# Loads over all 128 partitions: x, the rearranged Wo and the turned rows of a fused attention and gated-MLP kernel

## The chip, the cores and the metric

The kernel runs on one core of one Trainium2 chip. The metric is the device time of one execution in microseconds (us); the median over several runs counts. A core has five engines that run side by side: TensorE (PE, matrix multiplications; its weight loads are listed as PEld), VectorE (DVE), ScalarE (ACT), GpSimd (POOL) and SyncE (SP, which here only issues DMAs). Sixteen DMA engines move data between DRAM and on-chip memory (SBUF, 128 partitions). A DMA is issued by SP, ACT or POOL into that issuer's queue.

## The reference

Inputs are x (1 x 2048 x 640), wqkv (640 x 1920), wo (640 x 640), w_gate and w_up (640 x 1536) and w_down (1536 x 640), all bf16. The second x of the signature is not used.

```
xn = layernorm(x)
q, k, v = split(xn @ wqkv)                # 32 heads of 20
scores = q @ k^T * 20**-0.5               # causal, window of 256
a = (softmax(scores) @ v) @ wo
m = (sigmoid(xn @ w_gate) * (xn @ w_up)) @ w_down
out = x + a + m
```

## The kernel before

The 2048 rows are worked on in four chunks of 512 (`NCH`, `CW`); a chunk has four blocks of 128 rows (`SBC`). For a chunk the kernel needs the normalized rows with the model dimension on the partitions, `xnT[c]` (128 partitions x 4 blocks x 5 slices x 128 rows). The projections (`proj_block` for q and k, `both_v` and `project_v` for v) and the gate and up products (`g_gu`) all multiply with it.

Chunk 0 comes by four loads ahead of everything (`load_rows`) and is turned by TensorE. Chunks 1 to 3 go another way. `load_x(c)` loads the raw rows into a tile `xc` by four DMAs, DVE takes the statistics of each block (`ln_block`), POOL makes the reciprocal deviations (`rstds`), DVE normalizes in place and transposes squares of 32 x 32 (`turn_block`) into a tile `turn`. `turn_rows(c)` then finishes the turn through DRAM: it stores `turn` to a DRAM tile and loads `xnT[c]` from it, five DMAs on SP's queue. So that the 32 x 32 squares come out in the right place, `load_x` puts 32 consecutive rows of each block of 128 on each quarter of the partitions.

The output weights Wo are needed in an order of heads that differs from the input's. `turn_wo(r, side)` copies them piece by piece from DRAM to a DRAM tile `wo_i` by DMAs on POOL's queue (eight pieces of 80 rows), and `load_wo` loads the result into `wo`.

The heads' rows of q and k pass through DRAM as well: each projected block is copied from PSUM to a tile `st` (six buffers; DVE copies q, ACT copies k), stored to `scratch` (names sq and sk in the profile) and loaded in another layout (`spread`, tiles qT and kT). `clear` zeroes the padding rows of the scratch on POOL's queue; a small POOL copy, `landed`, reads the first loaded chunk 1 tile, so that the two clears are issued after that load.

TensorE's order is static. An outer loop walks the attention steps (scores of a step, L500; exponential on ACT, L506; masks on POOL and DVE; weighted values, L533, two steps later). Between them a planner (`Fill`) pulls other work from a list of labelled parts with their costs: gate and up products, projections of the next chunk, down projection and output (`g_out`: `down`, `add_wo`, `add_x`). DVE's share of the next chunk's normalization (`g_norms`) is mixed into these parts; `turn_rows(2)` and `load_x(3)` are reached while chunk 0's output is made. PSUM tiles of all these products rotate through four banks (`ps_d`). `new_rows` loads the rows of x that `add_x` adds (tile `rows`, three buffers).

SP works through its DMA issues in program order and waits at each for what that DMA needs. `load_x(1)` is issued ahead of chunk 0's q and k stores, `load_x(2)` among chunk 1's k stores, `turn_rows(2)` and `load_x(3)` ahead of two output stores and the rows of the third block.

Of the kernel before, what the change touches and what calls it, by code (L numbers as in the profile page):

```python
# [9 lines left out]
P = 128  # L10
S = 2048
D = 640
H = 32
DH = 20
F = 1536
DC = D // P
FC = F // P
CW = 512
NCH = S // CW
SBC = CW // P  # L20
HG = 4
NG = H // HG
# [13 lines left out]
BF16 = mybir.dt.bfloat16  # L36
# [33 lines left out]
def kernel(  # L70
# [11 lines left out]
    nc = tc.nc  # L82
    x2 = A_x.flatten_outer_dims()
# [27 lines left out]
    xc = {}  # L111

    def load_x(c):
        t = xp.tile([P, SBC, D], BF16, name="xc")
        xc[c] = t
        rows = x2[c * CW:(c + 1) * CW, :].rearrange("(a n t) d -> a t n d", a=SBC, n=SBC)
        for a in range(SBC):
            nc.sync.dma_start(out=t[32 * a:32 * a + 32], in_=rows[a])

    wqkv = const.tile([P, DC, 3 * D], BF16, name="wqkv")  # L120
    wqkv_r = A_wqkv.rearrange("(c p) n -> p c n", p=P)
# [3 lines left out]
    wo = const.tile([P, DC, D], BF16, name="wo")  # L125
# [28 lines left out]
    def clear(w):  # L154
        rows = scratch[w].rearrange("(h j) s -> h (j s)", j=32)[:, DH * CW:]
        nc.gpsimd.dma_start(out=rows.rearrange("h (a e) -> h a e", a=4), in_=zero[:, 0:3, :])
# [14 lines left out]
        for lo, hi in ((0, 3), (3, 6), (6, 8), (8, 10), (10, FC)):  # L171
            nc.sync.dma_start(out=wd[:, lo:hi, :], in_=wd_r[:, lo:hi, :])

    wo_i = tc.dram_tile([HG, NG * DH, D], BF16, name="wo_i")

    def turn_wo(r, side):
        to = wo_i.rearrange("i (r a d) n -> r a i (d n)", a=2, d=DH)
        rows = A_wo.rearrange("(a r i d) n -> r a i (d n)", a=2, i=HG, d=DH)
        nc.gpsimd.dma_start(out=to[r, side].rearrange("i (e w) -> e i w", e=16),
                            in_=rows[r, side].rearrange("i (e w) -> e i w", e=16))  # L180

    def load_wo():
        for i in range(HG):
            nc.sync.dma_start(out=wo[32 * i:32 * i + 32, :, :],
                              in_=wo_i[i].rearrange("(m j) n -> j m n", j=32))


    ident = const.tile([P, P], BF16, name="ident")
# [13 lines left out]
    xnT = {}  # L202
# [33 lines left out]
    turns = {}  # L236
# [8 lines left out]

    def turn_rows(c):
        xnT[c] = xtp.tile([P, SBC, DC, P], BF16, name="xnT")
        rows = tc.dram_tile([HG, P, D], BF16, name=f"turn{c}")
        nc.sync.dma_start(out=rows.rearrange("g p e -> p g e"), in_=turns[c].rearrange("p (g e) -> p g e", g=HG))
        for g in range(HG):  # L250
            nc.sync.dma_start(out=xnT[c][32 * g:32 * g + 32].rearrange("p a m t -> p a (m t)"),
                              in_=rows[g].rearrange("(a j) e -> j a e", j=32))

# [91 lines left out]
    def g_norms(c, turn):  # L347
        got = []
        yield from g_stats(c, got)
        yield 0  # L350
        for s in range(SBC):
            norm_rows(c, s, *got)
            yield 0
            turn_block(c, s)
            if turn and s == SBC - 1:
                turn_rows(c)
            yield 0
# [3 lines left out]
    def g_first(rstds):  # L361
        for s in range(0, SBC, 2):
            norm_rows(1, s, mvs1, rstds)
            norm_rows(1, s + 1, mvs1, rstds)
            yield 0
        for s in range(SBC):
            turn_block(1, s)
            if s == SBC - 1:
                turn_rows(1)
            yield 0  # L370
# [81 lines left out]
    def new_rows(c, s, name="rows", bufs=3, queue=nc.sync):  # L452
        rows = lnp.tile([P, D], BF16, name=name, bufs=bufs)
        queue.dma_start(out=rows, in_=xr[:, c * SBC + s, :])
        return rows
# [242 lines left out]
    banks.close()  # L698
    ps_s = banks.enter_context(tc.tile_pool(name="ps_s", bufs=1, space=bass.MemoryType.PSUM))
    load_x(1)  # L700
    load_gu(wg, B_w_gate, 0, FS // 2)
    landed = const.tile([P, 2], BF16, name="landed")
    nc.gpsimd.tensor_copy(out=landed, in_=xc[1][:, 0, 0:2])
    clear("q")
    clear("k")
    for k, _ in enumerate(g_qk(0)):
# [11 lines left out]
    def later(load, *args):  # L718
        load(*args)
        yield 0  # L720

    behind1 = {("qk"[n // 4], 1 + n % 4): (lambda n=n: turn_wo(n // 2, n % 2)) for n in range(2 * NP)}
    behind1["k", 0] = lambda: load_x(2)
    norms2 = itertools.chain(g_norms(2, True), later(load_x, 3))
    norms3 = g_norms(3, False)
    fill.add("gu0a", mix(g_gu(0, 0, 6), g_first(rstds1), 0), 6 * GU)
# [3 lines left out]
    fill.add("v1", mix(g_v(1), norms2, 2, 1, False), 40 * 136)  # L730
    fill.add("rest1", later(spread_rest, 1), 0)
    fill.add("wo", later(load_wo), 0)
    fill.add("gu0c", mix(g_gu(0, 9, 12), norms2, 0, 1, False), 3 * GU)
    fill.add("gu1a", mix(g_gu(1, 0, 2), norms2, 0, 1, False), 2 * GU)
    fill.add("out0", mix(g_out(0, g_gu(1, 2, 3)), norms2, 1, 1), OUT + GU)
    fill.add("qk2", mix(g_qk(2), norms3, 2, 1, False), 50 * MM)
    fill.add("v2", g_v(2), 40 * 136)
    fill.add("gu1b", mix(g_gu(1, 3, 12), norms3, 0, 2), 9 * GU)
    fill.add("turn3", later(turn_rows, 3), 0)
    fill.add("out1", g_out(1, g_gu(2, 0, 1)), OUT + GU)  # L740
    fill.add("qk3", g_qk(3), 50 * MM)
# [39 lines left out]
    c = NCH - 1  # L781
# [5 lines left out]
    rows = [new_rows(c, s, queue=nc.scalar) for s in range(SBC - 1)]  # L787
# [58 lines left out]
```

## Time and profile before

| what | value |
|---|---|
| median of 3 runs | 308.87 us (308.83 to 309.37) |
| the profiled execution | 309.65 us, of it span 308.0 us |
| TensorE clock granted | 1.00 |
| PE busy | 302.9 us, 98% of the span |
| DVE, ACT, POOL busy | 184.4, 193.2, 83.8 us |
| DMA | 36.86 MB, 120 GB/s over the span |
| xc loads, xnT loads, wo loads: median time from issue to landing | 4.0, 3.4, 9.1 us |

The span is the time from the first to the last instruction in the profile; the execution's own time lies 1.65 us above it. Times of single instructions are microseconds from the span's start. In a timeline a line reads: start, duration of the merged stretch, engine, line of the kernel, operation, what is written and read, how many, and in brackets the idle time ahead with what ended it. In a list of waits it reads: who waited, for whom, then the total in us, how many times, and the longest. In the DMA lines a queue has packets, megabytes, and the time that its packets took as a share of sixteen engines in the stretch asked for. The row of DMA digits gives the busy share of the DMA engines in 40 equal slices, in tenths.

### The profile page before, as it was taken

Reading aid. Unit: us, or ns where it says so; the run is one execution under the profiler, and the core shown is the slowest. Engines: PE = TensorE matmul, PEld = TensorE weight load, DVE = VectorE, ACT = ScalarE, POOL = GpSimd, SP = SyncE. Lnnn points to the kernel's source line nnn. Section 1 sums busy time; section 2 is a strip of 40 time slices with the busy share of each in tenths; the row PEclk is TensorE's granted clock in tenths of the full one; section 3 lists DMA queues with packets and bytes.
Section 4 is the critical chain, followed back from the end, with each engine's and each line's share of the span. In section 5 each row is a group of like instructions: output and inputs, shape, how many; then the busy total and the mean of one; then the engine's idle time right before and its main releaser. Section 6 shows DMA issues by size and latency. Waiting matters only on the chain.

```text
span 308.0 us, 10147 instructions
## 1 busy us (share of the span) xinstructions
PE 302.9 (98%) x4431; PEld 168.2 (55%) x4431; DVE 184.4 (60%) x378; ACT 193.2 (63%) x183; POOL 83.8 (27%) x189
## 2 busy tenths in 40 slices
PE   7999999999999999999999999999999999999996
PEld 3654445564456655654456655644546765444774
DVE  5787449298984579577642666454383627465523
ACT  6923785977766458867655557777766466778000
POOL 5011234635314133422213122241314132221100
PEclk9999999999999999999999999999999999999999
DMA  7997739889927222721152113550000210000301
GB/s 213 347 306 238 266 102 309 220 248 320 198 94 199 85 72 93 228 80 47 43 128 72 39 65 99 163 192 2 3 2 2 70 41 23 2 2 2 88 21 64
DMA packets 35756, 36.86 MB, mean 120 GB/s; under 512 B 2944, under 2 KB 35456, under 8 KB 35712
## 3 DMA queue, kind: packets, MB, share of 16 engines
q1 hardware_dynamic: 34304, 33.84, 36.6%
q0 software_dynamic: 544, 1.61, 1.7%
q10 hardware_dynamic: 864, 0.77, 0.9%
q8 instruction: 34, 0.56, 0.8%
q14 instruction: 10, 0.08, 0.1%
HBM read 25.59 MB, written 11.44 MB: 120 GB/s over the span
## 4 chain that ended last, share of the span: by engine, by line
PE 97%; DMA 1%; ACT 1%; DVE 0%; issue 0%; SPq 0%
PE pg L414 18%; PE y L437 18%; PE pu L423 17%; PE pqk L266 15%; PE ps L500 9%; PE y L444 7%; PE acc L533 6%; PE pv L324 6%; PE pv L304 1%; DMA xc<-in_A_x_dram 1%; PE pvh L304 0%; PE pt L233 0%; ACT turn L640 0%; ACT turn L645 0%; DVE turn L651 0%
## 5 line engine op out<-in xcount | busy, mean ns | idle before, releaser
L506 ACT ACTIVATE pT<-ps 128x2048 bf16<-128x2048 f32 x75 | 140.8, 1877 | 56.0 <-PE ps L500 33.4
L489 POOL TENSOR_SCALAR_AFFINE_SELECT pT<-pT 64x256 bf16<-64x256 bf16 (+1 forms) x126 | 67.5, 536 | 181.0 <-ACT pT L506 122.9
L414 PE MATMUL pg<-xnT,wg 128*128 128x512 bf16 x240 | 59.9, 380 | 0.0
L423 PE MATMUL pu<-xnT,wu 128*128 128x512 bf16 x240 | 59.8, 380 | 0.0
L427 DVE SCALAR_TENSOR_TENSOR h<-th,pu 128x512 bf16<-128x512 f32 x48 | 32.9, 685 | 42.8 <-ACT th L417 25.7
L437 PE MATMUL y<-wd,h 128*128 128x320 bf16 (+2 forms) x396 | 56.8, 295 | 0.0
L266 PE MATMUL pqk<-xnT,wqkv 128*128 128x512 bf16 x200 | 45.8, 381 | 0.0
L437 PEld LDWEIGHTS <-h 128*128 128x128 bf16 x396 | 36.8, 98 | 15.9 <-issue 2.3
L517 DVE TENSOR_TENSOR pT<-pT,keep 128x512 bf16<-128x512 bf16 (+2 forms) x81 | 35.4, 444 | 15.6 <-ACT pT L506 14.7
L417 ACT ACTIVATE th<-pg 128x512 f32<-128x512 f32 x48 | 28.6, 595 | 20.2 <-PE pg L414 19.9
L423 PEld LDWEIGHTS <-wu 128*128 128x128 bf16 x240 | 22.3, 98 | 27.3 <-issue 2.2
L414 PEld LDWEIGHTS <-wg 128*128 128x128 bf16 x240 | 21.7, 98 | 26.4 <-issue 2.9
L266 PEld LDWEIGHTS <-wqkv 128*128 128x128 bf16 x200 | 22.6, 119 | 19.0 <-issue 1.5
L500 PE MATMUL ps<-qT,kT 20*64 20x320 bf16 (+4 forms) x1440 | 32.0, 260 | 0.0
L544 DVE STREAM_TRANSPOSE t<-acc 128x512 f32<-128x512 f32 x32 | 21.0, 694 | 17.9 <-PE acc L533 17.9
L448 DVE SCALAR_TENSOR_TENSOR rows<-y,rows 128x320 bf16<-128x320 f32 x30 | 14.4, 489 | 24.2 <-PE y L444 24.2
L500 PEld LDWEIGHTS <-kT 20*64 20x64 bf16 x1440 | 13.5, 103 | 27.2 <-issue 26.7
L444 PE MATMUL y<-wo,oc 128*128 128x320 bf16 (+2 forms) x165 | 24.2, 295 | 0.0
L533 PE MATMUL acc<-pT,v 64*32 64x320 bf16 (+4 forms) x1440 | 20.3, 253 | 0.5 <-issue 0.5
L533 PEld LDWEIGHTS <-v 64*32 64x32 bf16 x1440 | 17.0, 92 | 4.2 <-issue 1.6
L444 PEld LDWEIGHTS <-oc 128*128 128x128 bf16 x165 | 15.5, 98 | 6.7 <-issue 1.0
L324 PE MATMUL pv<-wqkv,xnT 128*64 128x320 bf16 x240 | 17.4, 300 | 0.0
(61 smaller groups left out, 173.3 us busy)
## 6 DMA issues: line engine op xcount, KB each, us to landing
qT<-sq SPq DMA_DIRECT2D x16, 256.0 KB, 4.2
kT<-sk SPq DMA_DIRECT2D x16, 256.0 KB, 4.3
xc<-in_A_x_dram SPq DMA_DIRECT2D x16, 160.0 KB, 4.0
sq<-st SPq DMA_DIRECT2D x20, 128.0 KB, 3.6
sk<-st SPq DMA_DIRECT2D x20, 128.0 KB, 2.9
out_dram<-rows SPq DMA_DIRECT2D x15, 160.0 KB, 1.8
wg<-in_B_w_gate_dram SPq DMA_DIRECT2D x4, 480.0 KB, 7.2
wu<-in_B_w_up_dram SPq DMA_DIRECT2D x4, 480.0 KB, 7.4
```

Source lines behind the costliest of these rows:

```text
L266: nc.tensor.matmul(ps, lhsT=wt[:, m, :], rhs=xnT[c][:, :, d, :], start=(d == 0), stop=(d == DC - 1))
L324: nc.tensor.matmul(ps[hf * U:(hf + 1) * U, 0:HALF], lhsT=xnT[c][:, s, d, rows], rhs=wqkv[:, d, 2 * D + hf * HALF:2 * D + (hf + 1) * HALF], ...
L414: nc.tensor.matmul(pg, lhsT=part(wg, d, f), rhs=xnT[c][:, :, d, :], start=(d == 0), stop=(d == DC - 1))
L423: nc.tensor.matmul(pu, lhsT=part(wu, d, f), rhs=xnT[c][:, :, d, :], start=(d == 0), stop=(d == DC - 1))
L427: nc.vector.scalar_tensor_tensor(out=h, in0=th, scalar=1.0, in1=pu, op0=ADD, op1=MULT)
L437: nc.tensor.matmul(y[:, 0:cut[1] - cut[0]], lhsT=ht[c, f][:, s * P:(s + 1) * P], rhs=wd[:, f, cut[0]:cut[1]], start=(f == 0), stop=False)
L444: nc.tensor.matmul(y[:, 0:cut[1] - cut[0]], lhsT=oc[c, m][:, s * P:(s + 1) * P], rhs=wo[:, m, cut[0]:cut[1]], start=False, stop=(m == DC - 1))
L489: nc.gpsimd.affine_select(out=part, in_=part, pattern=pattern, compare_op=GE, fill=0.0, base=-1 if sign > 0 else 0, channel_multiplier=sign)
L500: nc.tensor.matmul(ps[side * U:(side + 1) * U, i, col * U:(col + n) * U], lhsT=qk["k", kc, half][32 * i:32 * i + DH, 2 * r + side, kb * U: ...
L506: nc.scalar.activation(out=pt[:, :, 0:used, :], in_=ps[:, :, 0:used * U], func=EXP, scale=SCALE)
L517: nc.vector.tensor_tensor(out=part, in0=part, in1=limit.to_broadcast([P, HG, n * U]), op=MIN)
L533: nc.tensor.matmul(accs[side][32 * i:32 * i + 32, q * U:(q + n) * U], lhsT=vt[sb][rows, b, at:at + 32], rhs=pt[rows, i, col:col + n, :], s ...
```

## The change

Four functions are edited and one line that reads a loaded tile.

- `load_x`: the four DMAs each filled 32 partitions with four stretches of 32 rows; now each fills one of the four column blocks on all 128 partitions.
- `turn_rows`: one store of `turn` over 128 partitions and four loads of 32 partitions; now four stores, one for each column group, and one load over 128 partitions.
- `turn_wo` and `load_wo`: `wo_i` now has the rows in the order in which `wo` wants them, so that `wo` is loaded by two DMAs over 128 partitions and not by four over 32. A piece of 20 rows that crosses a border of 32 is split, which makes 12 DMAs of the 8.
- `landed` reads the last column block of the tile, and so waits for the fourth DMA.

```diff
     def load_x(c):
         t = xp.tile([P, SBC, D], BF16, name="xc")
         xc[c] = t
-        rows = x2[c * CW:(c + 1) * CW, :].rearrange("(a n t) d -> a t n d", a=SBC, n=SBC)
-        for a in range(SBC):
-            nc.sync.dma_start(out=t[32 * a:32 * a + 32], in_=rows[a])
+        rows = x2[c * CW:(c + 1) * CW, :].rearrange("(a n t) d -> n a t d", a=SBC, n=SBC)
+        for n in range(SBC):
+            nc.sync.dma_start(out=t[:, n, :], in_=rows[n])
...
-    wo_i = tc.dram_tile([HG, NG * DH, D], BF16, name="wo_i")
+    wo_i = tc.dram_tile([D, D], BF16, name="wo_i")
 
     def turn_wo(r, side):
-        to = wo_i.rearrange("i (r a d) n -> r a i (d n)", a=2, d=DH)
-        rows = A_wo.rearrange("(a r i d) n -> r a i (d n)", a=2, i=HG, d=DH)
-        nc.gpsimd.dma_start(out=to[r, side].rearrange("i (e w) -> e i w", e=16),
-                            in_=rows[r, side].rearrange("i (e w) -> e i w", e=16))
+        to = wo_i.rearrange("(m i j) n -> m i (j n)", i=HG, j=32)
+        rows = A_wo.rearrange("(a r i d) n -> r a i (d n)", a=2, i=HG, d=DH)[r, side]
+        at, end = (2 * r + side) * DH, (2 * r + side + 1) * DH
+        first = at
+        while at < end:
+            m, j = divmod(at, 32)
+            n = min(end - at, 32 - j)
+            e = 16 if n == DH else n
+            nc.gpsimd.dma_start(
+                out=to[m][:, j * D:(j + n) * D].rearrange("i (e w) -> e i w", e=e),
+                in_=rows[:, (at - first) * D:(at - first + n) * D].rearrange("i (e w) -> e i w", e=e))
+            at += n
 
     def load_wo():
-        for i in range(HG):
-            nc.sync.dma_start(out=wo[32 * i:32 * i + 32, :, :],
-                              in_=wo_i[i].rearrange("(m j) n -> j m n", j=32))
+        rows = wo_i.rearrange("(m p) n -> p m n", p=P)
+        for lo, hi in ((0, 3), (3, DC)):
+            nc.sync.dma_start(out=wo[:, lo:hi, :], in_=rows[:, lo:hi, :])
...
     def turn_rows(c):
         xnT[c] = xtp.tile([P, SBC, DC, P], BF16, name="xnT")
-        rows = tc.dram_tile([HG, P, D], BF16, name=f"turn{c}")
-        nc.sync.dma_start(out=rows.rearrange("g p e -> p g e"), in_=turns[c].rearrange("p (g e) -> p g e", g=HG))
+        rows = tc.dram_tile([SBC * P, D], BF16, name=f"turn{c}")
+        to = rows.rearrange("(a g j) e -> g a j e", a=SBC, g=HG)
         for g in range(HG):
-            nc.sync.dma_start(out=xnT[c][32 * g:32 * g + 32].rearrange("p a m t -> p a (m t)"),
-                              in_=rows[g].rearrange("(a j) e -> j a e", j=32))
+            nc.sync.dma_start(out=to[g], in_=turns[c][:, g * D:(g + 1) * D])
+        nc.sync.dma_start(out=xnT[c].rearrange("p a m t -> p a (m t)"), in_=rows.rearrange("(a p) e -> p a e", p=P))
...
-    nc.gpsimd.tensor_copy(out=landed, in_=xc[1][:, 0, 0:2])
+    nc.gpsimd.tensor_copy(out=landed, in_=xc[1][:, SBC - 1, 0:2])
```

## The prediction

> **What bounds the kernel now.** I read the page first (busy time, the chain that ended last, the DMA lines), then TensorE's waits, then the DMA issues in time order, then the instructions that wait for them.
>
> From the page: busy time, the chain, the packets.
>
> ```profile
> PE 302.9 (98%) x4431; PEld 168.2 (55%) x4431; DVE 184.4 (60%) x378; ACT 193.2 (63%) x183; POOL 83.8 (27%) x189
> DMA  7997739889927222721152113550000210000301
> DMA packets 35756, 36.86 MB, mean 120 GB/s; under 512 B 2944, under 2 KB 35456, under 8 KB 35712
> PE 97%; DMA 1%; ACT 1%; DVE 0%; issue 0%; SPq 0%
> ```
>
> TensorE's own waits, in full:
>
> ```profile
> PE pwarm L199 <- PEq L830: 0.8, 1, 0.8
> PE pt L233 <- DVE turn L651: 0.7, 1, 0.7
> PE acc L533 <- issue: 0.5, 1, 0.5
> ```
>
> The end is set by TensorE at 97%, and after the start it waits for no DMA at all. So no faster load can shorten the run: its gain is capped near 0, while a transfer that grows past its slack costs its full excess. The DMA digits show little slack in the first 31 us and from 46 to 85 us (8 and 9 tenths).
>
> The edited transfers on SP's queue (start, time, what), and the packets' share of 16 engines in two stretches: the turn store alone (89 to 93 us), then four xnT loads with two rows loads (153 to 160):
>
> ```profile
> 10.28 1.76 SPq L118 DMA_DIRECT2D xc<-in_A_x_dram  x4
> 31.96 0.37 SPq L249 DMA_DIRECT2D turn<-turn  x1
> 37.70 2.99 SPq L251 DMA_DIRECT2D xnT<-turn  x4
> 97.34 0.43 SPq L454 DMA_DIRECT2D rows<-in_A_x_dram  x1
> q1 hardware_dynamic: 528, 0.66, 45.7%
> q1 hardware_dynamic: 864, 0.98, 58.7%
> ```
>
> The store over 128 partitions: 0.457 x 16 x 4 us = 29.2 us for 512 packets of 1280 B (16 more are end marks), 57 ns each. The second: 65.7 us, less 256 rows packets at 57 ns and 96 marks at about 10 ns, leaves 50 us for 512 packets into 32 partitions, 98 ns each. That is what the change can gain: 41 ns a packet, if sixteen engines still share it.
>
> **What the change does to each transfer.** Page: 2944 packets under 512 B. The issue list has 168 transfers; 168 x 16 = 2688, and the two smallest last stores (48 and 32 KB) add 128 + 128 short rows: 2944. So every transfer of before ended with a small mark from each of 16 engines. All had 16, 32 or 128 as outermost count on both sides. The wo_i stores, outermost count exactly 16, appear in the packet records as 1600 and 4800 B, together one index of that count per engine. The new x loads and turn stores count a = 4 outermost in DRAM (a, then 32 rows). No row shows such a count. Bounds: still 16 engines, or one share per index, 4 engines. I take 4, because the nearest row, wo_i, was handed out by whole indices and 4 leaves four.
>
> [...]
>
> With 4 engines, a group of four 160 KB transfers is 512 / 4 = 128 packets on each of the same four, and everything behind it in those queues waits. I take 60 ns a packet, just above 57 since neighbours are loaded: 7.7 us a group; bounds 55 and 98 ns, 7.0 and 12.5 us.
>
> **Place 1, load_x(1).** Who waits:
>
> ```profile
> POOL landed L703 <- DMA xc<-in_A_x_dram: 14.5, 1, 14.5
> ACT st L272 <- DMA sq<-st: 1.5, 1, 1.5
> 21.69 1.76 ACT L272 CAST st<-pqk 128x512 bf16<-128x512 f32 x3 [1.48 <-DMA sq<-st]
> 23.75 1.24 PE L414 MATMUL pg<-xnT,wg 128*128 128x512 bf16 x5
> ```
>
> Before, wu (issued at 6.5, 9.8 to landing) was in at 16.3 and the last x load at 19.1, just ahead of POOL's copy at 19.2: 2.8 us. Now 7.7, so what follows is 4.9 us late. The sq stores queue behind; ACT's copy of the second k block waits for the first sq store because st has six buffers, and its PSUM bank is the one that pg at 23.75 takes. That copy ends at about 22.3, a slack of 1.45. Stall: 4.9 - 1.45 = 3.4 us. With the clears' packets (2 us), now beside the sq stores, up to 5.4; at 55 ns with engines that are free earlier, 1.4.
>
> **Place 2, turn_rows(1).** The first user of the turned rows:
>
> ```profile
> 45.48 1.24 PE L266 MATMUL pqk<-xnT,wqkv 128*128 128x512 bf16 x5
> ```
>
> DVE follows TensorE, so the stores issue near 35.4. Ahead of them in the queues stand six qT/kT/wu/wg loads, before drained at 36.1; they move by about the 4.5 us of the late k stores, to 40.6. Four stores take 7.7 where one took 1.6: 48.3. The single load then costs what the lone 640 KB turn store did, 3.2 us from issue (four xnT loads: 5.4): 51.7 with the issue. Against 45.48 TensorE is then 6.2 us late in all, place 1 included.
>
> **Place 3, turn_rows(2) and load_x(3).**
>
> ```profile
> 102.69 0.88 DVE L448 SCALAR_TENSOR_TENSOR rows<-y,rows 128x320 bf16<-128x320 f32 x2
> 108.38 2.35 PE L266 MATMUL pqk<-xnT,wqkv 128*128 128x512 bf16 x10
> ```
>
> In times of before: stores from 89.9 end at 97.6 (92.2), the load at 101.0 (98.4), the x group at 108.7 (100.6), and the out store and rows load behind it (8 packets an engine each) at 109.6 (101.4). DVE wants those rows at 102.69: 6.9 late. Its first result, 0.49 later, frees the bank that pqk takes at 108.38, a slack of 5.2: 1.7 us more. DVE's masks stand behind that wait, but pv needs them only at 114.7.
>
> **What costs nothing.** load_x(2) at 56.5 ends 4 to 5 us later, near 67; its statistics run on DVE from 65.5 to 71.4, one block per load, and chunk 1's first scores at 78.0 have 6 us left. The SP queue behind, wd included, moves about 3 us; wd landed at 74.5 to 77.2 and is first used at 82.8, so at 7 us of delay this cover is gone and each further us costs one. wo is 640 packets over 128 partitions, 40 per engine: 40 x 41 ns = 1.6 us earlier and two issues fewer, against the 3 us; it landed at 86.1 and is used at 89.1, so 0 to 1 us. Turning Wo takes 12 POOL issues for 8: 4 x 0.53 = 2.1 us of POOL between 50 and 61 us, ahead of selects whose pv is two steps away; POOL is 27% busy. turn_rows(3) stores at 144.4 and its load waited until 153.7 anyway: covered up to 9 us. SP's issue count in turn_rows stays five. `landed` now waits for the fourth load alone, which is the last.
>
> **The sum.** 6.2 + 1.7 = 7.9 us. The profiled execution took 309.65 (span 308.0), so 317.55 for it; the median of the three runs is 0.78 below it: 308.87 + 7.9 = 316.8.
>
> **Rivals.** *Sixteen engines all the same* (not slower). The x group takes 32 x 57 ns = 1.8 us for 2.8, xnT and wo land earlier, and TensorE, which waits for none of it, does not notice: 308.9. For it: all 168 transfers used 16. Against: none had an outermost count of 4. It decides wherever a group stays under 2.8 + 1.45 = 4.3 us, 33 ns a packet on four engines, which no 1280 B row reaches.
>
> *The four engines get in each other's way.* Each then owns a block of 32 partitions, and 32 partitions is where the 98 ns rows come from. At 12.5 us a group: place 1 costs 9.7 - 1.45 = 8.3; place 2: queues drain 9.7 later than 36.1, stores to 58.3, load 61.5, 16.0 late in all; place 3 is 16.5 - 5.2 = 11.3: +27.3, 336. Against it: those rows had 16 engines on one block, not one. [...]
>
> *Slack swallows most*: four engines at 55 ns, no clears in the way. Place 1 1.4; place 2 drains 2.5 later (38.6), stores to 45.6, load 49.3, 3.8 late in all; place 3 nothing: 312.7. For it: many of these queues idle in between. Against: the 9s of the first 31 us.
>
> **How the numbers follow.** Chances: forecast 0.52; sixteen engines 0.12 (0.02 of it faster, since 0.5 us of issue idle could go; 0.09 the same, 0.01 slower); collision 0.18, spread over 320 to 336; slack 0.18, 0.02 of it the same. The forecast weighs most because whole indices are what the nearest row shows and 60 ns lies by the 57 of a transfer over all partitions. The range leaves out the sixteen engines, the last 0.02 and the collision's upper third, some 0.2: 311 to 331. Faster 0.02, same 0.11, slower 0.87; the bound is 0.2%, 0.6 us, about what a measurement of this kernel can tell from no change.
>
> **What would show it.** Small packets: the new kernel has 170 transfers, 2720 marks and 256 short rows on sixteen engines, 2976; on four, the 12 x loads and 12 turn stores lose 12 marks each: 2688. TensorE's waits should list pg or pqk with microseconds, xc landings of 9 us and more at 10.3, turn stores of 8 to 10 us, and DVE's rows waiting near 103. If the small packets count 2976 and xnT lands sooner, the four-engine step is wrong and with it the sign; if the marks are fewer and TensorE still waits for nothing, the slacks are.

## The result, and the profile after

The changed kernel takes 320.69 us (median of 6 runs, 317.97 to 321.7); the kernel before, run beside it, 308.94 (6 runs, 308.82 to 309.37). The ratio is 1.037, 95% interval 1.0327 to 1.0413: slower by 11.75 us. The profiled execution of the changed kernel took 317.97 (span 315.9), 8.3 above the profiled one of before. Of the six runs this is the only one with a granted clock of 1.000; the others have 0.984 to 0.995.

From the page of the changed kernel: busy time, the packets, and the chain that ended last.

```profile
PE 303.1 (96%) x4431; PEld 168.1 (53%) x4431; DVE 183.9 (58%) x378; ACT 192.8 (61%) x183; POOL 86.3 (27%) x193
DMA packets 35500, 36.86 MB, mean 117 GB/s; under 512 B 2736, under 2 KB 35184, under 8 KB 35456
PE 83%; DMA 10%; DVE 4%; SPq 2%; ACT 1%; issue 0%; DVEq 0%; ACTq 0%
```

TensorE does the same work (303.1 us busy, 302.9 before), but 10% of the chain is now DMAs. The packets under 512 B fell from 2944 to 2736, although there are two more transfers (170 for 168). All of TensorE's waits that are new, from its list of waits:

```profile
PE pqk L274 <- DVE rows L456: 3.3, 1, 3.3
PE pqk L274 <- DMA xnT<-turn: 2.7, 1, 2.7
PE pg L422 <- ACT st L280: 1.4, 1, 1.4
PE pu L431 <- DMA wu<-in_B_w_up_dram: 0.6, 1, 0.6
```

Together 8.1 us. With the 0.5 us of issue idle gone and 0.2 us more busy time that is 7.8 of the 7.9 us by which the span grew. They stand at the three places of the prediction. The SP queue there (start, time, what), and who waited, from the timelines:

```profile
10.31 4.36 SPq L118 DMA_DIRECT2D xc<-in_A_x_dram  x4
33.59 4.58 SPq L259 DMA_DIRECT2D turn<-turn  x4
45.77 0.37 SPq L260 DMA_DIRECT2D xnT<-turn  x1
108.38 0.43 SPq L462 DMA_DIRECT2D rows<-in_A_x_dram  x1
```

```profile
23.14 0.18 POOL L711 COPY landed<-xc 128x2 bf16<-128x2 bf16 x1 [18.43 <-DMA xc<-in_A_x_dram]
24.75 2.05 ACT L280 CAST st<-pqk 128x512 bf16<-128x512 f32 x4 [4.49 <-DMA sq<-st]
115.67 0.89 DVE L456 SCALAR_TENSOR_TENSOR rows<-y,rows 128x320 bf16<-128x320 f32 x2 [8.46 <-DMA rows<-in_A_x_dram]
116.22 2.32 PE L274 MATMUL pqk<-xnT,wqkv 128*128 128x512 bf16 x10 [3.33 <-DVE rows L456]
```

Place 1: the x group lands at 23.1 (19.2 before), ACT's copy waits for the sq store until 24.75 (21.69). Place 2: from the first turn store to the load behind the four, 33.6 to 45.8. Place 3: DVE waits 8.5 us for rows and passes 3.3 on to TensorE.

How many engines worked can be read directly. Chunk 2's four stores are alone on SP's queue from 95.5 to 103.8 us, and the packets' share of sixteen engines there is

```profile
q1 hardware_dynamic: 527, 0.65, 23.9%
```

0.239 x 16 = 3.8 engines. All four transfers had been issued by 97.0, and still no more than four engines were at work, so the four share the same ones.

### The profile page after: what moved, and what is told of

Read it like the earlier page. It is cut to its first block, busy times and chain, and to the rows that moved or that the text cites. A ratio compares the mean times of both kernels' runs of the same rounds, so it can differ in the third digit from the quotient of the medians.

```text
span 315.9 us, 10142 instructions
## 1 busy us (share of the span) xinstructions
PE 303.1 (96%) x4431; PEld 168.1 (53%) x4431; DVE 183.9 (58%) x378; ACT 192.8 (61%) x183; POOL 86.3 (27%) x193
## 2 busy tenths in 40 slices
DMA packets 35500, 36.86 MB, mean 117 GB/s; under 512 B 2736, under 2 KB 35184, under 8 KB 35456
## 4 chain that ended last, share of the span: by engine, by line
PE 83%; DMA 10%; DVE 4%; SPq 2%; ACT 1%; issue 0%; DVEq 0%; ACTq 0%
PE y L445 15%; PE pg L422 14%; PE pu L431 14%; PE pqk L274 12%; PE ps L508 8%; PE y L452 6%; PE acc L541 6%; PE pv L332 5%; DMA sq<-st 3%; DMA turn<-turn 3%; DMA rows<-in_A_x_dram 2%; DMA xnT<-turn 2%; PE pv L312 1%; SPq L259 1%; DVE turn L252 1%; DMA xc<-in_A_x_dram 1%
## 5 line engine op out<-in xcount | busy, mean ns | idle before, releaser
L274 PE MATMUL pqk<-xnT,wqkv 128*128 128x512 bf16 x200 | 45.8, 381 | 6.1 <-DVE rows L456 3.3
L280 ACT CAST st<-pqk 128x512 bf16<-128x512 f32 x20 | 11.1, 597 | 11.3 <-PE pqk L274 6.8
```

The lines of the kernel that those rows point to most:

```text
L274: nc.tensor.matmul(ps, lhsT=wt[:, m, :], rhs=xnT[c][:, :, d, :], start=(d == 0), stop=(d == DC - 1))
```

## The experiments

The line numbers shift with the edits; the functions are those of the change.

**One part alone.** `x_only` has the new `load_x` and `landed`, `turn_only` the new `turn_rows`, `wo_only` the new `turn_wo` and `load_wo`; the rest is the kernel before. The edits are the diff's own hunks.

> Only load_x and the line of landed as in the change; the turned rows and Wo as before. Theory (a share per outermost index, 4 engines a transfer): place 1 as in the changed kernel, 1.4 us at pg and 0.6 at pu behind wu; place 2 nothing, since the one store on 16 engines and its four loads end near 45.0 and TensorE, 2.0 late, wants them at 47.5; place 3 nothing, since the x group ends near 105.5 and the rows load behind it near 106.2, 3.5 late against a slack of 5.2. 308.9 + 2.0 = 310.9. Small packets: 12 x loads lose 12 marks each, 2944 - 144 = 2800. Rival (the x loads cost nothing, all of the loss is the turned rows'): 308.9. Clock: if TensorE's clock drops only after stalls near 3 us, it stays at 1.000 here.

Measured: 311.08 against 309.35 of before on that chip, ratio 1.006 (1.0039 to 1.0081), +1.7 us; expected +2.0. Small packets 2800, as expected. The profiled execution took 312.30, 1.2 us above the median. TensorE's largest new waits in it, and DVE's wait for rows:

```profile
PE pg L414 <- ACT st L272: 1.2, 1, 1.2
PE y L444 <- DMA wo<-wo_i: 1.0, 1, 1.0
PE pu L423 <- DMA wu<-in_B_w_up_dram: 0.9, 1, 0.9
DVE rows L448 <- DMA rows<-in_A_x_dram: 3.2, 1, 3.2
```

Place 1 is there, and DVE's 3.2 us for rows (expected 3.5) stop short of the slack of 5.2. One wait was not expected: with the old `load_wo`, whose four transfers write 32 partitions each, Wo comes 1.0 us late in this execution, where SP issues it 5 us later than in the kernel before (79.57 for 74.61). The waits for pg and pu make 2.1 us, the median's growth is 1.7, so the median run need not have had it. In the changed kernel this wait is missing. That the new wo load hides it there is likely, but not shown: TensorE also reaches Wo later there (at 93.6; here it would have at 90.8).

> Only turn_rows as in the change. Theory (4 engines a store): no stall at place 1; place 2: stores drain from 36.1 to 43.4 or 44, the load behind them took 4.9 us in the changed kernel, 48.5, so 3.0 us at the first pqk of chunk 1; place 3: stores end at 97.6, x group on 16 engines near 106, rows near 107, 4.3 late against a slack of 5.2, nothing. 308.9 + 3.0 = 311.9, a little more if the clock drops after the stall. Small packets: 3 x 4 stores of 4 marks and 3 loads of 16, 96 for 240 before, 2800. Rival (16 engines): 308.9 and 2944. The two single parts together then make 5.0 of the 7.9 us of the profile: place 3 needs both.

Measured: 312.92 against 309.35, ratio 1.0117 (1.0089 to 1.0145), +3.6 us. Small packets 2800, as expected; DVE waited 4.8 us for rows (expected 4.3), TensorE there not at all. Its one large wait, and the stretch and matmuls just behind it (the stretch's line gives its length, the busy time of PE, PEld, DVE, ACT and POOL with their instructions, and ends in TensorE's clock, the DMA share and GB/s):

```profile
PE pqk L266 <- DMA xnT<-turn: 1.7, 1, 1.7
49.40:52.90 3.50, 3.50 (x85) 1.94 (x78) 1.75 (x3) 1.88 (x1) 1.36 (x3) 0.51 1.11 342
51.12 3.17 PE L266 MATMUL pqk<-xnT,wqkv 128*128 128x512 bf16 x10
```

The wait was 1.7 and not 3.0 us, but in the 3.5 us after the first matmuls the clock was 0.51. Ten pqk matmuls took 3.17 us (2.35 at full clock) and the 72 weighted-value matmuls (`acc`) ahead of them 1.80 (1.03): 1.6 us more. The trace's clock rows put the drop at 49.43, for 3.41 us.

The two parts alone make 5.3 us together and the whole change 11.75. The other 6.4 us need both groups in one queue; the last experiments look for them at place 3.

> Only turn_wo and load_wo as in the change. Theory: nothing on TensorE's path, 308.9 within 0.3, TensorE waits for no DMA; the wo loads land some 1.6 us sooner, near 84.5. Rival (four more POOL issues delay the selects, or the clock term): 309.5 or more.

Measured: 309.46 against 309.35, ratio 1.0011 (0.9992 to 1.0029): no difference, and TensorE waits for no DMA after the start. POOL's four more issues cost nothing. Small packets are 3024, 48 above the count of marks and short rows, 2976: POOL's queue has 48 extra packets of 16 B. Six of the split pieces have an outermost count of 12, 8 or 4, two of each, and 2 x (4 + 8 + 12) = 48 is the number of engines that a share per index would leave with nothing to move. POOL's queue still shows 16 marks for every transfer (224 for 14), so there the marks do not tell how many engines moved data. The changed kernel's 2736 is the predicted 2688 and these 48.

**Sixteen engines, with the single load.**

```diff
-        to = rows.rearrange("(a g j) e -> g a j e", a=SBC, g=HG)
-        for g in range(HG):
-            nc.sync.dma_start(out=to[g], in_=turns[c][:, g * D:(g + 1) * D])
+        to = rows.rearrange("(a g j) e -> a j g e", a=SBC, g=HG)
+        for a in range(SBC):
+            nc.sync.dma_start(out=to[a], in_=turns[c][32 * a:32 * a + 32].rearrange("p (g e) -> p g e", g=HG))
```

with `load_x` and `landed` as before.

> Wo as in the change; load_x as before; turn_rows stores by quarter of the partitions (outermost counts 32 on both sides) and loads once over 128 partitions. Every transfer then has 16 engines. Theory of the outermost count: 308.9 within 0.3, no DMA wait on TensorE, the single load kept; if the stores read 32 partitions at the 98 ns that loads show, the store group takes 3.1 us for 1.8, which the slack of 2.3 covers. Rival (it is the single load behind four stores, whatever the engine count, that is late): 2 us or more at the first pqk of chunk 1, 311 or more.

Measured: 309.36 against 309.35, ratio 0.9997 (0.9986 to 1.0008). The load is issued at 38.62 and no longer at 45.77, and chunk 2's stores, alone in the stretch from 89 to 95 us, show their price:

```profile
38.62 0.38 SPq L260 DMA_DIRECT2D xnT<-turn  x1
q1 hardware_dynamic: 576, 0.66, 46.4%
```

0.464 x 16 x 6 = 44.5 us, less 64 marks, for 512 packets: 86 ns each, against 57 over 128 partitions; the slack covers it. So at place 2 neither the single load nor the four stores cost time: the outermost count does. This form is level with the kernel before and cannot beat it, since TensorE waits for no DMA there. A form of `load_x` over all 128 partitions with sixteen engines was not run.

**A count of two.** The kernel before, but for chunk 3 alone:

```diff
+        if c == NCH - 1:
+            rows = tc.dram_tile([SBC * P, D], BF16, name=f"turn{c}")
+            to = rows.rearrange("(a g j) e -> g a j e", a=SBC, g=HG)
+            for half in (0, 1):
+                for g in range(HG):
+                    nc.sync.dma_start(out=to[g, 2 * half:2 * half + 2], in_=turns[c][64 * half:64 * half + 64, g * D:(g + 1) * D])
+            nc.sync.dma_start(out=xnT[c].rearrange("p a m t -> p a (m t)"), in_=rows.rearrange("(a p) e -> p a e", p=P))
+            return
```

> The kernel before, but chunk 3's turned rows are stored by eight transfers of 64 partitions each, whose DRAM side counts 2 outermost, and loaded once. Theory (a share per outermost index): two engines take all 512 packets, 256 x 57 ns = 14.6 us from some 145.8, the load is issued near 160.5 and not at 153.7; small packets 2944 - 80 + 8 x 2 + 16 = 2896. Chunk 3 is wanted only at 179 and the rows loads behind it have 5.2 us of bank slack, so the time stays 309.3 within 0.6, with two engines overloaded. Rival (count 2 is spread over 16 engines): small packets 3008 and a load still issued at 153.7. Second rival (any group on few engines costs, wherever it stands): 2 us or more on TensorE.

Measured: 310.03 against 309.56, ratio 1.0017 (0.9992 to 1.0042), no clear difference. The packets, SP's queue, and the packets' share from 145 to 161 us:

```profile
DMA packets 35708, 36.86 MB, mean 120 GB/s; under 512 B 2896, under 2 KB 35408, under 8 KB 35664
144.03 8.49 SPq L253 DMA_DIRECT2D turn<-turn  x8
160.86 0.36 SPq L254 DMA_DIRECT2D xnT<-turn  x1
q1 hardware_dynamic: 528, 0.66, 12.1%
```

2896 and 160.86, where 2896 and 160.5 were expected, and 0.121 x 16 = 1.9 engines at work: two shares, two engines. And a load issued 7 us later than in the kernel before (153.67) brings no clear loss where the slack is larger.

**Place 3 and the clock.** `after_again` is the changed kernel beside the next three. `warm` adds work where TensorE waits for the first turned rows:

```diff
         ps = ps_d.tile([P, CW], FP32, name="pqk", tag="d")
+        if (w, c, m) == ("q", 1, 0):
+            for k in range(12):
+                nc.tensor.matmul(ps, lhsT=ones[:, 0:P], rhs=ones, start=(k == 0), stop=(k == 11))
```

`x3_late` takes the x group away from place 3:

```diff
-    norms2 = itertools.chain(g_norms(2, True), later(load_x, 3))
+    norms2 = g_norms(2, True)
...
+    fill.add("x3", later(load_x, 3), 0)
     fill.add("qk2", mix(g_qk(2), norms3, 2, 1, False), 50 * MM)
```

> The changed kernel itself, beside the others on one chip. Theory of the remainder (its six runs lie 0.0, 2.0, 2.0, 3.5, 3.5 and 3.7 us above the profiled one, with granted clocks of 1.000, 0.995, 0.995, 0.989, 0.984 and 0.984; 3.41 us at half clock over the span is 0.005, so 0, 1, 1, 2, 3 and 3 such windows after the stalls): a median near 320.5, and a profile with a clock under 1 shows windows of 3.41 us at 0.5 behind the stall at chunk 1's first pqk or chunk 2's. Rival (the DMAs vary from run to run): longer stalls at a clock of 1.000.

Measured: 319.38 against 309.27, ratio 1.0321 (1.0277 to 1.0366). Its profile (319.51, clock 0.989) has the clock at half from 113.70 for 6.83 us, twice 3.41. The drop comes inside the 3.6 us (111.8 to 115.4) in which TensorE idles for DVE's rows:

```profile
115.38 4.42 PE L274 MATMUL pqk<-xnT,wqkv 128*128 128x512 bf16 x10 [3.59 <-DVE rows L456]
116.50:120.00 3.50, 3.50 (x24) 1.08 (x22) 1.98 (x5) 0.00 (x0) 0.00 (x0) 0.50 0.31 109
```

The ten matmuls take 4.42 us where the first profile shows 2.32. In the clock rows the stretches between two changes are whole multiples of the shortest one, 3.41 us (13, 1 and 76 in `turn_only`: 44.37, 3.41 and 259.41 us; 91 in the first profile: 310.61 us), so the changes seen lie on a grid of 3.41 us. In `turn_only` the drop came behind a stall of 1.7 us. These are the windows of the grid that hold most of a stall, in `turn_only` (46.01), here (110.28) and in the first profile (114.29):

```profile
46.01:49.42 3.41, 1.67 (x30) 0.70 (x32) 1.30 (x3) 0.25 (x1) 0.74 (x2) 1.00 1.06 365
110.28:113.69 3.41, 1.51 (x33) 0.89 (x31) 0.00 (x0) 1.82 (x2) 0.92 (x2) 1.00 0.28 101
114.29:117.70 3.41, 1.48 (x7) 0.82 (x7) 1.33 (x4) 0.56 (x1) 1.33 (x2) 1.00 0.35 107
```

TensorE was busy for about half of each. The clock fell at the end of the first two and not of the third. Where the grid cut a stall into smaller shares (1.5 and 1.3 us at the first profile's place 2) it did not fall either. So how a stall lies on the grid seems to matter, but the third window shows that this does not decide alone; what does is open.

> The changed kernel with 12 more matmuls over a constant, into the bank of chunk 1's first pqk, which then overwrites them; 12 x 0.216 = 2.6 us, inside the 2.7 us that TensorE waits there for the turned rows. Theory (the clock drops because TensorE idles there): the window behind this stall goes, the median falls by one window's cost, 1.5 to 2 us, to some 319, though work was added; what is left comes from the stall at chunk 2's first pqk. Rival (the median's excess is varying DMA time): 320.5 or, with stalls shorter than 2.6 us, more.

Measured: 321.24, ratio 1.0363 (1.0332 to 1.0395): the fall to 319 did not come, and the median is 1.9 us above the unwarmed kernel's, with overlapping intervals. By the numbers on record the rival fits better. The profiles show that the place was badly chosen: neither profile of the unwarmed kernel has a drop at chunk 1's pqk that the 12 matmuls could have removed, and the warmed one has its drop at 118.38 behind chunk 2's, where TensorE idled 3.7 us. So this run leaves open whether the idling causes the drops.

> The changed kernel with load_x(3) issued after chunk 0's output, not ahead of the rows load of its third block. Theory of place 3 (the rows load stands behind the x group in four engines' queues): the wait of DVE for rows goes from 8.5 us to under 1, TensorE's 3.3 us at chunk 2's first pqk go, and the clock windows behind it: 320.5 - 3.3 - 1.5 to 2 = 315.5, more by up to 2 if DVE now waits for chunk 3's rows. Rival (the stall there comes from turn_rows(2) alone): 319 or more, with the wait for rows still over 5 us.

Measured: 315.95, ratio 1.0199 (1.0165 to 1.0234), 3.4 below `after_again`; expected 315.5. DVE's wait for rows and TensorE's largest wait:

```profile
DVE rows L456 <- DMA rows<-in_A_x_dram: 2.1, 1, 2.1
PE pqk L274 <- DMA xnT<-turn: 2.5, 1, 2.5
```

8.5 became 2.1, not under 1; the wait of chunk 2's pqk for DVE is gone. Place 3 is the x group ahead of the rows load.

> Both edits. Theory: no idle stretch of TensorE over 1.5 us is left, the clock is 1.000 in nearly every run, and the time is the old one and the stalls alone: 308.9 + 1.4 + 0.6 + 2.7 = 313.6, runs close together. Rival (DMA variation): as x3_late, spread over 2 us or more.

Measured: 314.9, ratio 1.0176 (1.0148 to 1.0204), 1.3 above the expected 313.6. The runs lie between 314.52 and 315.73, those of `x3_late` between 314.13 and 316.86. Three of the six runs of `x3_late` have a clock of 0.993 to 0.995 and take 316.62 to 316.86; all five of the warmed kernel have 0.999 or 1.000. Both profiles have a clock of 1.000, that of the warmed kernel 0.6 us longer. This is what a removed window looks like, but the intervals overlap and the runs are few: not settled.

## Why the prediction was right

The sign, the mechanism and the three places held; 320.69 lies inside 311 to 331, and the 7.9 us of the sum met 7.9 of the profiled span. That hit is partly luck, since place 2's total was 1.0 us too high and place 3's 1.6 too low, and the 0.5 us of issue idle that went was not in the sum.

- *TensorE waits for no DMA, so nothing can be gained*: right. `wo_only` and `by_quarter` shorten some transfers and end within 0.2%.
- *A share per outermost index, four engines*: right on SP's queue. 2800 marks and short rows in each single part, 2896 for a count of two, and 3.8 and 1.9 engines at work. That the four transfers of a group all go to the same four engines, as the 7.7 us assume, no run of before shows; the 3.8 engines, measured when all four transfers had been issued, show it for the changed kernel's stores. Which of the sixteen they are, no row shows.
- *7.7 us a group*: chunk 2's stores, issued at 94.28, were followed by the load at 103.76. In that stretch (94 to 104 us) the packets' share is

```profile
q1 hardware_dynamic: 528, 0.66, 19.9%
```

  0.199 x 16 x 10 = 31.8 us, 62 ns a packet for the 60 taken. From 111.5 to 115 us, where most packets are those of chunk 3's x loads, the share is

```profile
q1 hardware_dynamic: 290, 0.35, 28.1%
```

  0.281 x 16 x 3.5 = 15.7 us for 276 packets and 14 marks, 57 ns a packet. That is also what became of the collision rival: four blocks of 32 partitions on an engine each cost 57 to 62 ns, not 98.
- *Place 1, 3.4 us*: measured 1.4, the bound given for "engines that are free earlier". The x group was 3.9 us late at POOL's copy and the ACT copy 3.1, not 4.9. A second wait of 0.6 us, pu behind wu, was not in the sum.
- *Place 2, 6.2 us in all*: 50.71 - 45.48 = 5.2. The stores were done at about 45.7, 2.6 sooner than reckoned; the load took 4.9 and not 3.2. The time of the stores was set too late and the load too short, so two errors partly cancel. For the load, a store of the same bytes was the wrong row (`by_quarter`: 4.2 to 5.4). Its 3.2 us also enters as 3.4 in the forecast, 3.2 in the collision sum and 3.7 in the slack sum; that moves them by 0.5 us at most.
- *Place 3, 1.7 us*: 3.3. DVE waited 8.5 for rows, not 6.9; less the slack of 5.2 that is 3.3, so the step held. The x group was sized well: from the load's issue at 103.76 to DVE's start on the rows at 115.67 it took 11.9 us for the 12.0 reckoned (97.6 to 109.6). What was under-sized is the stores ahead of it, 9.5 us from the first issue to the load's for 8.6 (89.02 to 97.6), and they were issued 5.3 us later than before (94.28 for 89.02), while DVE wanted its rows only 4.5 later (107.21 for 102.69).
- *wo costs 0 to 1 us*: it cost nothing, and `wo_only` shows no difference. That the new form saved the 1.0 us of `x_only`'s profile is not shown.
- *The median follows from the profile by 0.78*: this failed, and is the 3.9 us between 316.8 and 320.69. The sum held the clock at 1. Five of the six runs had it at 0.984 to 0.995, and one window is worth up to 1.7 us (3.41 at half rate); `turn_only` measured 1.6 for one. How many windows each run had is read from its mean clock, not seen. The clock need not be all of it: the two runs at 0.995, one window, lie 2.0 us above the run at 1.000, and the eight runs of `x_only` spread over 2.0 us at clocks of 0.999 and 1.000. The rival of DMA times that vary from run to run is not excluded.

## What to carry to other kernels

"All 128 partitions" says nothing on how many DMA engines work: look at the outermost count of both sides. Here turn stores whose DRAM side counted 4 had 3.8 engines at work and those that counted 2 had 1.9, while the transfers of the kernel before, with 16, 32 or 128 on both sides, left a mark from each of sixteen (2688 for 168). For transfers issued by SP the small end packets went with the engines at work (four for each of the 12 x loads in `x_only`, 2800 for 2944 in all; two for each of the eight stores in `turn3_two`, 2896); for those of POOL they did not, with 224 marks for 14 transfers in `wo_only`. A group on few engines was paid for by what stood behind it in the same queue, beyond the slack of that follower: at place 3 DVE waited 8.5 us for rows, 5.2 of them were slack, and TensorE lost 3.3. And a stall of TensorE may come with a stretch at half clock, as after 1.7 us in `turn_only`, where it cost 1.6 us, and in the 3.6 us of `after_again`; a single profile can miss it, as the first one did, with a stall of 3.3 us at a clock of 1.000.

## What the runs showed of the hardware

- SP took longer to issue a transfer for few engines: in the median 0.60 us for an x load and 0.56 for a turn store on four engines (changed kernel), against 0.43 for an x load (kernel before) and 0.44 for a store (`by_quarter`) on sixteen. Single groups took much longer: the first four x issues 4.36 us (1.76 before), the eight stores for two engines 8.49 (`turn3_two`). SP's next issue, of wg behind the first x group, is later by as much: 14.71 for 12.09.
- With sixteen engines on one block of 32 partitions a packet of 1280 B took 86 ns in stores (`by_quarter`) and 98 in loads (kernel before), against 57 in a store over 128 partitions (kernel before). With four engines on a block of 32 partitions each it took 57 to 62 (changed kernel).
- The clock fell to half for 3.41 us (`turn_only`) or twice that (`after_again`), on a grid of 3.41 us. It fell once behind 1.7 us of idle time (`turn_only`), and another time, with 3.3 us, it did not (the first profile of the changed kernel). Runs with such a mean clock occur without the new stalls as well, but seldom: of the 12 runs of `wo_only` and the 17 of the kernel before beside `turn3_two`, two each have 0.994.
